# Mixture scores and values as fp32 products in quarters of the array, with exchanged halves and both tails together

## The chip, the cores and the metric

The kernel runs on one core of one Trainium2 chip. The metric is device time in microseconds: the median of three runs of the kernel before is 472.44 us (471.9 to 473.13). PE is TensorE, DVE is VectorE, ACT is ScalarE, POOL is GpSimd, and SP is the engine whose queue issues most of the loads and stores.

## The reference

Windowed attention (8 batches, 8 heads, 576 rows, head size 64), whose output is the input of a mixture of four causal attentions with gates:

```python
scores = scale * q @ k.T + slope[h] * -abs(i - j)      # attention: only 0 <= i - j < 128
x = softmax(scores) @ v                                # heads side by side: x is 576 x 512
logits = x @ w_gate                                    # the two largest of four get weights w
for e in range(4):                                     # mixture: experts of size 64
    q, k, v = x @ wq[e], x @ wk[e], x @ wv[e]
    a = softmax(causal(scale * q @ k.T))
    out += w[:, e] * (a @ v @ wo[e])                   # only where e is among the two
```

All inputs and outputs are fp32.

## The kernel before, in words

The 576 rows of a batch are four blocks of 128 and a tail of 64. Two heads, or two experts, make a pair, one in each half of the 128 partitions. Attention of a batch is four groups of two heads. Then the mixture of the batch runs: projections to Q and K (`qkproj`) and to V with the gates (`vproj`), scores of a pair (`moe_s`) and of its tail (`moe_s_tail`), norms and gate weights (`moe_norm`), transposes of the probabilities (`moe_t`), the product with V (`moe_pv`, `moe_pv_tail`), and the output product (`moe_wo`).

PE works with numbers in two ways. An fp32 product has two records in the trace for each instruction. An fp32r product is one record, and where its precision is not enough the kernel splits each factor into a high and a low part and adds three products (high by high, low by high, high by low): `WH`, `WL` for weights, `QH`, `QL`, `KH`, `KL` for Q and K, `AH`, `AL` for the result of `moe_pv`. The array is used whole (128*128), in two halves (64*128 by rows, 128*64 by columns) or in four quarters (64*64), and products on different parts of it run side by side. Quarters are used before in attention's scores and values; the mixture's scores are fp32r in row halves, the score tails fp32r on the whole array (through `QJ`, a block diagonal of two tails of Q), the mixture's values fp32 in column halves.

The helpers that choose an engine are `evac` (copy out of PSUM on ACT or DVE), `rnd` (rounding to fp32r on POOL or ACT), `ssub` (the low part, DVE or POOL) and `dve_sub` (the same out of PSUM, DVE only). All eight banks of PSUM are one pool (`ps`), SBUF tiles of one width another (`w5`: 1344 columns, `w4`: 1024, `w2`: 512); a tile takes the buffer that came free first in the final order.

The kernel first records all operations. `plan` then puts them in an order that is written out as a packed table (`ORDER`): it gives the place of every operation in one list, which of the alternative engines runs it, and where an idle product (`fill`) is put in on PE. `place` gives the buffers. Each engine runs its part of that list from first to last, and waits where a factor, a buffer or a bank is not ready. So every recorded operation has one line in the profile, L1189, and the clearing of the banks L1187.

At the start DVE clears part of each bank (192 columns of the upper 64 partitions), PE runs `fill` products into the banks (`warm`), and attention's scores of the first four groups begin as soon as their head data arrive; the four weight blocks (`wall`) are loaded behind the head data, rounded and split (`wprep`).

Of the kernel before, what the change touches and what calls it, by code (L numbers as in the profile page):

```python
# [20 lines left out]
DM = H * D  # L21
E = 4
# [8 lines left out]
BIG = 3.0e38  # L31
EPS = 1e-9
# [1244 lines left out]
```

## Time and profile before

| | |
|---|---|
| median of three runs | 472.44 us |
| the profiled execution's own time | 473.2 us |
| its span | 471.4 us |
| busy: PE, DVE, ACT, POOL | 462.7, 409.3, 370.5, 222.7 us |
| granted clock of PE, mean | 0.998 |

The span runs from the first to the last recorded work. A busy time is the union of the instructions of an engine; on PE they overlap, since a product's record runs from its first column to its last result, so a product's price is read from the distance of two starts and not from one record's length. An instruction's row gives what its engine waited for before it, in square brackets, where the wait was seen.

### The profile page before, as it was taken

The numbers are of one execution on the slowest core, as the hardware profiler recorded it, in microseconds if no ns is written. First come the engines' busy times: TensorE is split into PE (matmuls) and PEld (weight loads), VectorE is DVE, ScalarE is ACT, GpSimd is POOL, SyncE is SP. The second block draws the span as 40 slices with busy tenths as digits, with TensorE's granted clock in tenths as the row PEclk, the third lists the DMA queues.
The fourth block names the chain that finished last, engine by engine and source line by source line (L and its number), as shares of the span: only waits on it lengthen the run. The fifth ranks groups of instructions, "written<-read, shape, count | busy, mean of one in ns | idle before, by whom it ended". The sixth has DMA issues, their size and how long they took to land.

```text
span 471.4 us, 17542 instructions
## 1 busy us (share of the span) xinstructions
PE 462.7 (98%) x6380; PEld 403.8 (86%) x6380; DVE 409.3 (87%) x1894; ACT 370.5 (79%) x1409; POOL 222.7 (47%) x464
## 2 busy tenths in 40 slices
PE   7999999999999999999999999999999999999996
PEld 5788999897889789797898987898789897899775
DVE  6999999979998998879989798798999979966852
ACT  5968879989978688796989798897976959833952
POOL 4833968183916346261470907426263623561430
PEclk9999999999999999999999999999999999999999
DMA  7899410345320653150441281602731030300033
GB/s 202 266 221 246 112 52 1 77 103 141 108 80 0 139 142 117 29 140 1 115 129 37 80 189 39 180 2 61 205 121 38 3 86 2 120 1 1 3 113 112
DMA packets 29862, 44.99 MB, mean 95 GB/s; under 512 B 9424, under 2 KB 15824, under 8 KB 29776
## 3 DMA queue, kind: packets, MB, share of 16 engines
q1 hardware_dynamic: 29040, 43.42, 34.0%
q8 instruction: 50, 0.82, 0.8%
q10 hardware_dynamic: 736, 0.46, 0.4%
q14 instruction: 36, 0.29, 0.2%
HBM read 34.42 MB, written 9.44 MB: 93 GB/s over the span
## 4 chain that ended last, share of the span: by engine, by line
PE 84%; DMA 5%; SPq 3%; DVE 3%; ACT 2%; POOL 1%; issue 1%; DVEq 0%
PE ps L1189 84%; DMA w<-in_hd 4%; SPq L1189 3%; DVE w L1189 2%; ACT w L1189 2%; POOL w L1189 1%; DMA w<-in_wall 1%; DVE ps L1189 1%; DVE WL L1189 0%; DVE ALm L1189 0%; ACT AHm L1189 0%; DVE mr L1189 0%; DVE nm L1189 0%; POOL QJm L1189 0%; DVE ALTm L1189 0%
## 5 line engine op out<-in xcount | busy, mean ns | idle before, releaser
L1189 ACT COPY w<-ps 128x256 f32<-128x256 f32 (+2 forms) x232 | 92.4, 443 | 29.8 <-PE ps L1189 21.3
L1189 PE MATMUL ps<-wx,WH 128*128 128x288 f32 (+2 forms) x512 | 110.4, 300 | 0.0
L1189 ACT ACTIVATE w<-w,nm 128x128 f32<-128x128 f32 x252 | 98.9, 397 | 7.3 <-DVE nm L1189 5.8
L1189 POOL TENSOR_SCALAR w<-w,mr,w 128x256 f32<-128x256 f32 (+3 forms) x128 | 78.2, 622 | 43.2 <-DVE mr L1189 24.1
L1189 POOL TENSOR_SCALAR w<-w,r 128x128 f32<-128x128 f32 x177 | 64.6, 378 | 68.3 <-PE ps L1189 25.4
L1189 PEld LDWEIGHTS ps<-wx,WH 128*128 128x128 f32 x512 | 83.2, 190 | 1.5 <-issue 0.3
L1189 ACT ACTIVATE w<-w,mnm 128x512 f32<-128x512 f32 (+3 forms) x128 | 71.2, 558 | 10.0 <-DVE mnm L1189 9.4
L1189 DVE TENSOR_TENSOR w<-ps,tmt 128x768 f32<-128x768 f32 (+3 forms) x96 | 72.5, 770 | 3.3 <-PE ps L1189 2.2
L1189 DVE CUSTOM_DVE_ANT_0 w<-ps,tbt 128x128 f32<-128x128 f32 x288 | 71.7, 283 | 1.1
L1189 PE MATMUL ps<-wx,WL 128*128 128x288 f32 (+2 forms) x256 | 71.9, 298 | 0.0
L1189 PE MATMUL ps<-WH,wx 128*128 128x260 f32 x288 | 61.5, 285 | 0.0
L1189 PE MATMUL ps<-w 64*64 64x192 f32 (+3 forms) x1256 | 58.6, 304 | 2.3 <-DMA w<-in_hd 1.7
L1189 PE MATMUL ps<-idt,w 64*128 64x64 f32 (+1 forms) x1152 | 58.6, 230 | 1.0 <-POOL w L1189 0.9
L1189 PEld LDWEIGHTS ps<-idt,w 64*128 64x128 f32 (+1 forms) x1152 | 47.4, 139 | 11.0 <-issue 3.4
L1189 PE MATMUL ps<-w,vt 64*64 64x192 f32 (+3 forms) x1344 | 56.3, 283 | 0.0
L1189 PEld LDWEIGHTS ps<-w,vt 64*64 64x64 f32 (+1 forms) x1344 | 50.0, 133 | 5.7 <-DVE r L1189 0.6
L1189 DVE COPY_PREDICATED ps<-mkt,ps 128x128 f32<-128x128 int32 (+2 forms) x160 | 49.2, 329 | 5.4 <-PE ps L1189 5.0
L1189 PEld LDWEIGHTS ps<-w 64*64 64x64 f32 (+1 forms) x1256 | 44.0, 134 | 8.6 <-DMA w<-in_hd 2.7
L1189 DVE CUSTOM_DVE_ANT_0 w<-ps,mtt 128x256 f32<-128x256 f32 (+2 forms) x96 | 49.8, 551 | 0.8 <-PE ps L1189 0.4
L1189 PEld LDWEIGHTS ps<-WH,wx 128*128 128x128 f32 x288 | 48.0, 189 | 0.8 <-issue 0.3
L1189 ACT ACTIVATION_READ_ACCUMULATOR w<-w,nm 128x1 f32 x252 | 48.6, 193 | 0.0
L1189 PE MATMUL ps<-w,w 128*64 128x64 f32 (+4 forms) x576 | 48.0, 319 | 0.0
(111 smaller groups left out, 947.5 us busy)
## 6 DMA issues: line engine op xcount, KB each, us to landing
w<-in_hd SPq DMA_DIRECT2D x56, 288.0 KB, 4.6
vt<-in_vd SPq DMA_DIRECT2D x28, 320.0 KB, 3.7
out<-w SPq DMA_DIRECT2D x31, 256.0 KB, 2.5
w<-in_hd SPq DMA_DIRECT2D x14, 128.0 KB, 3.5
w<-in_hd SPq DMA_DIRECT2D x56, 32.0 KB, 3.7
w<-in_wall SPq DMA_DIRECT2D x4, 386.0 KB, 6.6
out<-w SPq DMA_DIRECT2D x8, 128.0 KB, 3.3
vt<-in_vd SPq DMA_DIRECT2D x4, 192.0 KB, 3.8
```

What stands on the lines that cost most here:

```text
L1189: getattr(getattr(tc.nc, e), m)(*a, **k)
```

## The change

Q and K of the mixture stay plain fp32 (`KK`), without high and low parts. Scores are single fp32 products in quarters: for block i, each half of 64 rows of Q runs only over the keys that it may see, so one half is 64 columns shorter than the other; in odd blocks the two halves are exchanged (`y ^ i & 1`), with a second mask table (`mts`) whose halves are exchanged too. The score tails of both pairs are one operation of each batch, fp32 in quarters. The transposes put the exchanged halves back (`spread`), the tails' transposes are five blocks in halves, and the gates' weights of odd blocks are computed with exchanged halves. `moe_pv` runs in quarters into two banks, whose sum is formed by a copy, an addition, a rounding and a subtraction; `moe_pv_tail` does so for both pairs at once. In attention's first half the first two blocks of a group run without wrapping (`first_blocks`). Pools change: `w5` has nine buffers for eight, `w4` six for four, `w2` five for six, `w1` goes. The weights are prepared in two parts each. The banks are cleared more widely, `ORDER` is another table (not shown), and the profile's lines become L1227 and L1224/L1225.

```diff
-    pp = big5 = _Slots(cp, 8, 2 * S + 3 * D, "w5")
+    pp = big5 = _Slots(cp, 9, 2 * S + 3 * D, "w5")
     tp = big10 = _Slots(cp, 3, 2 * (S + TAIL + S), "w10")
-    tw = _Slots(cp, 4, 2 * DM, "w4")
-    tr = _Slots(cp, 3, P, "w1")
-    big2 = _Slots(cp, 6, DM, "w2")
+    tw = _Slots(cp, 6, 2 * DM, "w4")
+    big2 = _Slots(cp, 5, DM, "w2")
...
+    mts = cp.tile([P, NQ * P], BF16, name="mts")
...
+    def first_blocks(g, ss, q, k, tb):
+        nm, sm, pt = state[g, 0]
+        for i in range(2):
+            n = P + P * i
+            for h in range(2):
+                d = slice(D * h, D * h + D)
+                for y in range(2):
+                    m = P * i + D * y
+                    nc.tensor.matmul(
+                        ss[h][D * y : D * y + D, P * i : P * i + n], q[h][d, m : m + D], k[d, :n], start=True, stop=True
+                    )
...
-    QJ = m1.tile([P, 2, 2, P], F32R, name="QJm")
     MPL = [m1.tile([P, (NQ + 1) * P], F32, name=f"MPL{k}") for k in range(2)]
-    QH, QL = (m1.tile([P, 2, S], F32R, name=f"{n}m") for n in ("QH", "QL"))
-    KK = m1.tile([P, 2, 2, S], F32R, name="KKm")
-    KH, KL = KK[:, 0], KK[:, 1]
+    KK = m1.tile([P, 2, 2, S], F32, name="KKm")
...
+    def terms(late):
+        return sorted(((c, j) for c in range(4) for j in range(3)), key=lambda z: late and z[1] == 2)
...
-        hi, lo = (QH, QL) if isq else (KH, KL)
-        act_copy(hi[:, pr, sl], o, n)
-        dve_sub(lo[:, pr, sl], o, hi[:, pr, sl].bitcast(F32), n)
-        if isq and half == 1:
-            for x, q in ((0, QH), (1, QL)):
-                for j in range(2):
-                    d = slice(D * j, D * j + D)
-                    pool_round(QJ[d, pr, x, d], q[d, pr, S - TAIL :].bitcast(F32))
+        evac(KK[:, 0 if isq else 1, pr, sl], o)
...
-        terms = ((QH, KH), (QL, KH), (QH, KL))
         o = 0
         jobs = []
         for i in blocks:
             n = P * (i + 1)
-            m = n if i else 2 * P
-            for x, (q, k) in enumerate(terms if i else terms[:2]):
-                for j in range(2):
-                    d = slice(D * j, D * j + D)
-                    k2 = k[d, pr, :n] if i else KK[d, :, pr, :P]
+            for j in range(2):
+                d = slice(D * j, D * j + D)
+                for y in range(2):
+                    m = P * i + D * (y ^ i & 1)
                     nc.tensor.matmul(
-                        ss[j][:, o : o + m], q[d, pr, P * i : P * (i + 1)], k2, start=(x == 0), stop=(x == (2 if i else 1))
+                        ss[j][D * y : D * y + D, o : o + m + D], KK[d, 0, pr, m : m + D], KK[d, 1, pr, : m + D], start=True, stop=True
                     )
-            if i == 0:
-                for j in range(2):
-                    nc.vector.tensor_tensor(st["pk", pr, j][:, :P], ss[j][:, :P], mtt[:, 512 - P : 512], add)
-                o += P
...
-                softmax_block(ss[j][:, o : o + n], pt, mtt[:, 512 - n : 512] if i else pt, nm[:, c : c + 1], n)
+                softmax_block(ss[j][:, o : o + n], pt, (mts if i % 2 else mtt)[:, 512 - n : 512], nm[:, c : c + 1], n)
...
-    def moe_s_tail(b, pr):
+    def moe_s_tail(b):
         st = m2s[b]
-        nm, sm = st[pr, "nm"], st[pr, "sm"]
-        pt = MPL[pr]
         ss = []
+        stats(b, 1)
         for half in range(2):
-            s = ps_s.tile([P, 512], F32, tag="s", name=f"msl{b}_{pr}_{half}")
-            ss.append(s)
+            ss.append([ps_s.tile([P, 512], F32, tag="s", name=f"msl{b}_{half}_{j}") for j in range(2)])
             sl = slice(HALF * half, HALF * (half + 1))
-            for k, (x, w) in enumerate(((0, KH), (1, KH), (0, KL))):
-                nc.tensor.matmul(s[:, :HALF], QJ[:, pr, x, :], w[:, pr, sl], start=(k == 0), stop=(k == 2))
...
+            for j in range(2):
+                d = slice(D * j, D * j + D)
+                for pr in range(2):
+                    nc.tensor.matmul(
+                        ss[half][j][D * pr : D * pr + D, :HALF], KK[d, 0, pr, NQ * P :], KK[d, 1, pr, sl], start=True, stop=True
+                    )
...
-    def moe_pv(b, pr, c):
+    def moe_pv(b, pr):
         st = m2s[b]
-        if c == 0:
-            st["acc"] = ps_a.tile([P, 512], F32, tag="m" if K["M"] else "a", name=f"ma{b}_{pr}", bufs=K["M"] or K["A"])
-        acc = st["acc"]
+        xa, ya = (ps_a.tile([P, 512], F32, tag="m", name=f"{n}{b}_{pr}") for n in ("ma", "mb"))
...
-        n = 512 - P * c
-        for j in range(2):
-            e = 2 * pr + j
-            nc.tensor.matmul(
-                acc[D * j : D * j + D, P * c :], V2[:, c, D * e : D * e + D], st["pt"][pr, j, c][:, :n],
-                start=(c == 0), stop=True, skip_group_check=True,
-            )
-        if c == NQ - 1:
-            act_copy(AH[:, pr, :512], acc, 512)
-            dve_sub(AL[:, pr, :512], acc, AH[:, pr, :512].bitcast(F32), 512)
-
-    def moe_pv_tail(b, pr):
+        for c in range(NQ):
+            for y, dst in enumerate((xa, ya)):
+                r, f = slice(D * y, D * y + D), D * y
+                for j in range(2):
+                    e = 2 * pr + j
+                    nc.tensor.matmul(
+                        dst[D * j : D * j + D, P * c + f :], V2[r, c, D * e : D * e + D], st["pt"][pr, j, c][r, f : 512 - P * c],
+                        start=(c == 0), stop=True, skip_group_check=True,
+                    )
+        tmp = big2.tile([P, DM], F32, tag="xs", name=f"ma{b}_{pr}t")
+        evac(tmp, xa)
+        nc.vector.tensor_tensor(tmp[:, D:], tmp[:, D:], ya[:, D:], add)
+        rnd(AH[:, pr, :512], tmp)
+        ssub(AL[:, pr, :512], tmp, AH[:, pr, :512].bitcast(F32))
+
+    def moe_pv_tail(b):
         st = m2s[b]
         pt = st["pt"]
         V2 = st["v2"]
-        acc = ps_t.tile([P, 512], F32, tag="t", name=f"mal{b}_{pr}")
+        ta, tb_ = (ps_t.tile([P, 512], F32, tag="t", name=f"mal{b}_{y}") for y in range(2))
         for c in range(NQ + 1):
-            for j in range(2):
-                e = 2 * pr + j
-                src = pt[pr, "tail", c][:, D * j : D * j + D]
-                nc.tensor.matmul(
-                    acc[D * j : D * j + D, :TAIL], V2[:, c, D * e : D * e + D], src,
-                    start=(c == 0), stop=(c == NQ),
-                )
+            for y, dst in enumerate((ta, tb_) if c < NQ else (ta,)):
+                r = slice(D * y, D * y + D)
+                for pr in range(2):
+                    for j in range(2):
+                        e = 2 * pr + j
+                        nc.tensor.matmul(
+                            dst[D * j : D * j + D, D * pr : D * pr + D], V2[r, c, D * e : D * e + D], pt[j, "tail", c][r, D * pr : D * pr + D],
+                            start=(c + pr == 0), stop=True, skip_group_check=True,
+                        )
         o = TAIL * (b % 2)
-        ht, lt = AHT[:, pr, o : o + TAIL], ALT[:, pr, o : o + TAIL]
-        act_copy(ht, acc[:, :TAIL], TAIL)
-        dve_sub(lt, acc[:, :TAIL], ht.bitcast(F32), TAIL)
+        ht, lt = AHT[:, :, o : o + TAIL], ALT[:, :, o : o + TAIL]
+        tt = p2.tile([P, P], F32, tag="xq2", name=f"xm{b}")
+        evac(tt, ta[:, :P])
+        nc.vector.tensor_tensor(tt, tt, tb_[:, :P], add)
+        v = tt.rearrange("p (a n) -> p a n", n=TAIL)
+        rnd(ht, v)
+        ssub(lt, v, ht.bitcast(F32))
...
             nc.sync.dma_start(mtt, mt)
+            for y in range(2):
+                nc.sync.dma_start(mts[D * y : D * y + D], mt[D - D * y : 2 * D - D * y, : NQ * P])
...
+            for f in (slice(0, 4 * P), slice(4 * P, NW)):
+                w, hi, lo = wst[c][:, f], WH[:, NP_ - 1 - c, f], WL[:, NP_ - 1 - c, f]
+                rnd(hi, w)
+                ssub(lo, w, hi.bitcast(F32))
+            return
...
-    fetch(0, 1, 0)
+    for g in range(4):
+        fetch(g, 1, 0)
     nc.scalar.dma_start(idt, ident)
-    nc.scalar.dma_start(tmt, tm)
-    nc.scalar.dma_start(mkt[:, P:], mk[:, P:])
...
     warm()
-    fetch(1, 1, 0)
     fetch_v(0, 0)
-    fetch(2, 2, 0)
     fetch_v(1, 0)
+    wload(0)
     fetch_v(2, 0)
-    wload(0)
     fetch_v(3, 0)
     for c in range(1, 4):
         wload(c)
+    nc.sync.dma_start(tmt, tm)
+    nc.sync.dma_start(mkt[:, P:], mk[:, P:])
...
+        moe_s_tail(b)
+        moe_norm(b, 0, 2)
+        moe_norm(b, 1, 2)
...
-        tc.nc.vector.memset(t[D:, : 3 * P].rearrange("p (a n) -> p a n", n=P)[:, :, :D], 0.0)
+        tc.nc.vector.memset(t[D:], 0.0)
+        tc.nc.vector.memset(t.rearrange("p (a n) -> p a n", n=4 * D)[:D, :, D : 2 * D], 0.0)
```

On SP, the order of loads at the start (`hd`: head data, `rd`: its query tails, `vd`: values, `mt`: mask table) begins before with

```order
L1189 DMA w_90<-in_hd 64x2x256 x4
L1189 DMA w_91<-in_hd 64x2x256 x4
L1189 DMA w_90<-in_hd 128x2x128
L1189 DMA w_90<-in_rd 128x2x320
L1189 DMA w_90<-in_hd 64x2x256 x2
```

and now with

```order
L1227 DMA mts<-in_mt 64x512 x2
L1227 DMA w_91<-in_hd 64x2x256 x4
L1227 DMA w_92<-in_hd 64x2x256 x4
L1227 DMA w_91<-in_rd 128x2x320
L1227 DMA w_91<-in_hd 64x2x256 x2
```

Two loads of the mask table stand ahead of all head data. The next rows of the same queue hold the four weight blocks (`in_wall`); before:

```order
L1189 DMA w_83<-in_wall 128x772
L1189 DMA vt_128<-in_vd 128x256
L1189 DMA vt_129<-in_vd 128x256
L1189 DMA w_86<-in_wall 128x772
L1189 DMA w_87<-in_wall 128x772
L1189 DMA vt_130<-in_vd 128x256
L1189 DMA vt_131<-in_vd 128x256
L1189 DMA w_88<-in_wall 128x772
```

and now:

```order
L1227 DMA vt_126<-in_vd 128x256
L1227 DMA vt_125<-in_vd 128x256
L1227 DMA w_83<-in_wall 128x772
L1227 DMA w_84<-in_wall 128x772
L1227 DMA mkt<-in_mk 128x64
L1227 DMA w_91<-in_hd 128x2x128
L1227 DMA vt_127<-in_vd 128x256
L1227 DMA vt_128<-in_vd 128x256
L1227 DMA w_85<-in_wall 128x772
L1227 DMA w_92<-in_rd 128x2x320
L1227 DMA w_92<-in_hd 128x2x128
L1227 DMA w_86<-in_wall 128x772
```

The fourth weight block was the 20th load of the queue and is the 25th.

On PE, a mixture pair's scores (blocks 3 and 2) in the middle of the program, with numbers of tiles and banks, before:

```order
L1189 MATMUL ps7_76<-KKm_125,QHm_123 128x512
L1189 MATMUL ps4_73<-KKm_125,QHm_123 128x512
L1189 MATMUL ps7_76<-KKm_125,QLm_124 128x512
L1189 MATMUL ps4_73<-KKm_125,QLm_124 128x512
L1189 MATMUL ps7_76<-KKm_125,QHm_123 128x512
L1189 MATMUL ps4_73<-KKm_125,QHm_123 128x512
L1189 MATMUL ps2_71<-KKm_125,QHm_123 128x384
L1189 MATMUL ps3_72<-KKm_125,QHm_123 128x384
L1189 MATMUL ps2_71<-KKm_125,QLm_124 128x384
L1189 MATMUL ps3_72<-KKm_125,QLm_124 128x384
L1189 MATMUL ps2_71<-KKm_125,QHm_123 128x384
L1189 MATMUL ps3_72<-KKm_125,QHm_123 128x384
```

and now, with the value product (`w41,w56`: probabilities and V) that stands behind it:

```order
L1227 MATMUL ps1_70<-KKm_122 64x512
L1227 MATMUL ps1_70<-KKm_122 64x448
L1227 MATMUL ps4_73<-KKm_122 64x512
L1227 MATMUL ps4_73<-KKm_122 64x448
L1227 MATMUL ps3_72<-KKm_122 64x320
L1227 MATMUL ps3_72<-KKm_122 64x384
L1227 MATMUL ps5_74<-KKm_122 64x320
L1227 MATMUL ps5_74<-KKm_122 64x384
L1227 MATMUL ps0_69<-w41_95,w56_88 64x512 x2
L1227 MATMUL ps7_76<-w41_95,w56_88 64x448 x2
L1227 MATMUL ps0_69<-w45_99,w56_88 64x384 x2
L1227 MATMUL ps7_76<-w45_99,w56_88 64x320 x2
```

Twelve products of 128 output rows became eight of 64, the longer half first in block 3 and second in block 2; the value product follows in the same tile size and takes two banks.

## Rows read from the trace of the kernel before

**Rows 1.** The page's first part: busy time, share of the span, instructions.

```profile
PE 462.7 (98%) x6380; PEld 403.8 (86%) x6380; DVE 409.3 (87%) x1894; ACT 370.5 (79%) x1409; POOL 222.7 (47%) x464
```

**Rows 2.** Busy time by stretch; columns: stretch, length, engines, clock, DMA share, GB/s.

```profile
0.00:25.00 25.00, 21.70 (x209) 17.23 (x209) 20.58 (x111) 17.40 (x71) 15.73 (x26) 1.00 0.84 236
...
100.00:200.00 100.00, 100.00 (x1503) 86.37 (x1504) 92.88 (x422) 81.73 (x305) 48.98 (x107) 1.00 0.35 92
200.00:300.00 100.00, 99.33 (x1406) 88.62 (x1399) 86.63 (x411) 85.69 (x331) 49.71 (x105) 1.00 0.36 95
300.00:400.00 100.00, 99.37 (x1405) 86.55 (x1405) 91.75 (x423) 81.26 (x315) 39.84 (x88) 1.00 0.26 74
```

**Rows 3.** The two holes: PE's timeline, then the chain (start, length, what).

```profile
284.45 0.60 PE L1189 MATMUL ps<-w 64*64 64x128 f32 x10 [0.67 <-DMA w<-in_hd]
...
335.05 4.65 DMA w<-in_hd
```

**Rows 4.** PE's timeline, quarters of attention; start, length, engine, operation, wait.

```profile
12.77 1.53 PE L1189 MATMUL ps<-w 64*64 64x192 f32 x32
14.23 0.87 PE L1189 MATMUL ps<-idt,w 128*128 128x128 f32 x5
```

**Rows 5.** PE's timeline, a pair's value product and what follows.

```profile
158.17 2.37 PE L1189 MATMUL ps<-w,w 128*64 128x512 f32 x16
160.47 0.33 PE L1189 MATMUL ps<-idt,w 128*128 128x128 f32 x1
...
160.91 0.29 PE L1189 MATMUL ps<-wx,WH 128*128 128x288 f32 x1
161.04 0.29 PE L1189 MATMUL ps<-KKm,QJm 128*128 128x288 f32 x1
```

**Rows 6.** PE's timeline, first score product of a pair and first work behind it.

```profile
217.83 0.50 PE L1189 MATMUL ps<-KKm,QHm 64*128 64x512 f32 x2
...
219.85 0.33 PE L1189 MATMUL ps<-idt,w 128*128 128x128 f32 x1
```

**Rows 7.** Groups by shape: busy us and mean ns, then idle before.

```profile
L1189 PEld LDWEIGHTS ps<-w 64*64 64x64 f32 x1248 | 42.8, 134 | 7.8 <-DMA w<-in_hd 2.7 <-issue 1.1 <-DVE G L1189 0.9
L1189 ACT COPY w<-ps 128x512 f32<-128x512 f32 x99 | 56.1, 590 | 16.2 <-PE ps L1189 15.4
L1189 POOL TENSOR_TENSOR wx<-w,wx 128x512 fp32r<-128x512 f32 x17 | 22.2, 1309 | 0.5
L1189 DVE TENSOR_TENSOR w<-w,ps 128x448 f32<-128x448 f32 x28 | 17.1, 612 | 1.2 <-ACT w L1189 0.6 <-PE ps L1189 0.2 <-issue 0.2
L1189 POOL TENSOR_SCALAR wx<-w 128x512 fp32r<-128x512 f32 x19 | 11.8, 624 | 27.5 <-DVE w L1189 23.1 <-ACT w L1189 3.7 <-DVE ps L1189 0.3
L1189 DVE TENSOR_TENSOR ALm<-ps,AHm 128x512 fp32r<-128x512 f32 x16 | 11.0, 686 | 1.1 <-ACT AHm L1189 0.8
L1189 DVE TENSOR_TENSOR wx<-w,wx 128x512 fp32r<-128x512 f32 x11 | 9.7, 877 | 1.2 <-ACT wx L1189 0.7 <-POOL wx L1189 0.4
L1189 ACT CAST AHm<-ps 128x512 fp32r<-128x512 f32 x14 | 8.1, 578 | 5.1 <-PE ps L1189 5.0
L1189 DVE MEMSET MPL<- 128x64 f32 x2 | 0.2, 112 | 0.0
```

**Rows 8.** The start, by engine: timelines of DVE, PE, SP and POOL.

```profile
0.85 1.67 DVE L1187 MEMSET ps<- 64x192 f32 x8 [0.85 <-PEq L1262]
...
1.30 3.57 PE L1189 MATMUL ps<-QJm 128*128 128x256 f32 x15 [1.30 <-DVE ps L1187]
4.81 3.69 PE L1189 MATMUL ps<-w 64*64 64x128 f32 x52
...
16.79 0.49 PE L1189 MATMUL ps<-wx,WH 128*128 128x256 f32 x2
...
0.73 5.97 SPq L1189 DMA_DIRECT2D w<-in_hd  x9
...
18.00 0.84 POOL L1189 TENSOR_SCALAR WH<-w 128x772 fp32r<-128x772 f32 x1 [0.65 <-DMA w<-in_wall]
```

More of the change, by code (lines that the diff above doesn't have):

```diff
@@ L31 @@
 BIG = 3.0e38
+NEG = -8.0e9
 EPS = 1e-9
@@ L312, in attn_moe_kernel @@
     prepped = {}
+    half = {}
     SM = [cp.tile([P, 9, 2], F32, name=f"sm{k}") for k in range(2)]
@@ L739, in qkproj, with stats @@
         o = acc[:, :n]
[L740 to L741 removed]
+        for k, (c, j) in enumerate(terms(b == 0 and half == 0)):
             xh, xl = xT[4 * b + c]
             cw = c if b else NP_ - 1 - c
[L744 to L757 removed]
+            lhs, rhs = ((WH, xh), (WH, xl), (WL, xh))[j]
+            nc.tensor.matmul(
+                o, lhs[:, cw, P * mtile : P * (mtile + 1)], rhs[:, n0:n1], start=(k == 0), stop=(k == 11)
+            )
+        sl = slice(n0, n1)
+        evac(KK[:, 0 if isq else 1, pr, sl], o)
+    def stats(b, pr):
+        st = m2s[b]
+        if (pr, "nm") not in st:
+            st[pr, "nm"] = m1.tile([P, 11], F32, tag=f"mnm{pr}", name=f"mnm{b}_{pr}")
+            st[pr, "sm"] = MSM[pr]
     def moe_s(b, pr, blocks):
@@ L761, in moe_s @@
         if blocks[0] == 0:
-            st[pr, "nm"] = m1.tile([P, 11], F32, tag=f"mnm{pr}", name=f"mnm{b}_{pr}")
-            st[pr, "sm"] = MSM[pr]
+            stats(b, pr)
             for j in range(2):
@@ new lines, in moe_s_tail @@
+            for j in range(2):
+                nm = st[j, "nm"]
+                bias = mtt[:, 0:HALF] if half == 0 else mtt[:, 512:]
+                init = BIG if half == 0 else nm[:, 9:10]
+                dst = nm[:, 9:10] if half == 0 else nm[:, 8:9]
+                softmax_block(ss[half][j][:, :HALF], MPL[j][:, sl], bias, dst, HALF, init=init)
+        for j in range(2):
+            nm, sm = st[j, "nm"], st[j, "sm"]
+            for half in range(2):
+                sl = slice(HALF * half, HALF * (half + 1))
+                exp_block(ss[half][j][:, :HALF], MPL[j][:, sl], nm[:, 8:9], sm[:, 16 + half : 17 + half], HALF)
+            st["p"][j, "tail"] = MPL[j]
@@ L836, in moe_t @@
         st = m2s[b]
-        parts = ([(0, 0), (1, 0)], [(0, 1), (0, 3), (1, 1), (1, 3)], [(0, 2), (1, 2)], [("tail", c) for c in range(NQ)])[u]
-        n = 8 if u < 2 else 4
-        pc = (tw if u < 2 else big2).tile([P, n * P], F32, tag="pt", name=f"mpt{b}_{pr}_{u}")
+        parts = ([(0, 0), (1, 0)], [(0, 3), (0, 1), (1, 1), (1, 3)], [(0, 2), (1, 2)], [("tail", c) for c in range(NQ + 1)])[u]
+        n = (8, 8, 4, 5)[u]
+        pc = (big2 if u == 2 else tw).tile([P, n * P], F32, tag="pt", name=f"mpt{b}_{pr}_{u}")
         blocks = []
@@ L943, in wload @@
             nc.sync.dma_start(mtt, mt)
+            for y in range(2):
+                nc.sync.dma_start(mts[D * y : D * y + D], mt[D - D * y : 2 * D - D * y, : NQ * P])
         wst[c] = w
@@ L1000, in f @@
             if tail:
-                moe_pv_tail(b, pr)
+                moe_pv_tail(b)
             else:
-                for c in range(NQ):
-                    moe_pv(b, pr, c)
+                moe_pv(b, pr)
             live[0] -= 0 if tail else 7
@@ L1127, in su @@
             else:
[L1128 removed]
+                u.append((0.1, early(lambda: first_norm(g))))
                 if g % 2:
```

328 lines of the change are left out of this document (162 added, 166 removed).

## The prediction

> **What bounds the kernel now.** I read the page's first part, then busy time in stretches, then TensorE's timeline. The first line says PE 98% busy, VectorE 87%, ScalarE 79%, GpSimd 47% [rows 1]. By stretches PE is busy 21.70 of the first 25 us, all of 100 to 200, 99.33 of 200 to 300 and 99.37 of 300 to 400, at a granted clock of 1.00 throughout, so at the upper of its two levels, 2.4 GHz [rows 2]. PE lists instructions as busy while they overlap, so 98% alone could hide gaps; but starts follow each other at the instructions' own rate, and outside the start only two holes show, of 0.67 and 0.63 us by the stretches, and both stand behind loads of head data [rows 2, 3]: the first is PE's wait at 284.45, the second is a load of 4.65 us on the chain of waits from 335.05. So the time is PE's work, plus what the first 25 us lose (3.30 us), plus 1.3 us of holes, plus what follows the last product. Shorter work on VectorE or ScalarE is worth nothing by itself.
>
> **Prices on PE.** Two rows give the fp32 price. The 32 records of 192 columns between 12.77 and 14.23 are 4 products for each quarter (two records each): 768 columns in 1.46 us [rows 4]. The 16 records of a value product between 158.17 and 160.47 run 512+384+256+128 = 1280 columns in each half: 2.30 us [rows 5]. The difference is 0.84 us for 512 columns, 1.64 ns a column, and leaves 0.20 us a stretch, which is what a change of tile size costs (going in and coming out). An fp32r step of 288 columns is 0.13 us (160.91 to 161.04) [rows 5]. One pair's fp32r scores, 11 steps, take 2.02 us from 217.83 to 219.85, so 1.82 without the change of size [rows 6].
>
> **The change, part by part (8 batches, 2 pairs each).**
> - Scores: each quarter now runs 512+320+256+64 or 448+384+192+128 = 1152 columns, 1.89 us against 1.82; 16 × 0.07 = +1.1.
> - The two quarters that write one bank differ by 64 columns in a block. If PE issues in order and every block ends with its longest, 128 columns a pair are lost, 0.21 us; if the shorter runs ahead, none. 0 to +3.4; I take +1.7, since the exchange makes the sums equal over two blocks but the queue need not reach that far.
> - Score tails: six steps for each pair were 2 × 6 × 0.13 = 1.56 us a batch; now 2 × 288 columns in four quarters, 0.94. 8 × -0.62 = -4.9.
> - Values: the busier row half still runs 1280 columns, and the tails ten times 64 for both pairs where each pair ran five: 0. The second bank only moves the sum of the halves to VectorE.
> - Attention's first half: 64 more columns a quarter in four groups, 4 × 64 × 1.64 ns = +0.4. The order of PE holds 32 more transposes of 64 columns and 8 fewer of 128, which I put at +0.2.
> - Tile sizes: scores, tails and values now stand side by side in one size; in the two orders of PE I count 153 changes of size before and 131 now. 22 × 0.20 = -4.4; some fall in the start, where PE waits anyway, so -4.0.
> Work on PE: +1.1 +1.7 -4.9 +0.4 +0.2 -4.0 = -5.5, with ends -7.2 and -3.8.
>
> **Other engines.** VectorE loses 64 subtractions of some 288 columns (each shorter than the 0.69 of a 512 wide one) and 32 additions of 128, and gets 16 additions of 448 at 0.61, 9.8 us, and part of 16 subtractions of 512; it becomes lighter by 20 to 30 us of 409. GpSimd gets up to 16 × (0.62 + 1.31) = 31 us on its 223, and ScalarE keeps its load within a few us [rows 1, 7]. All this lies beside PE and I cost it at nothing; the cover would be gone only where PE waits for one particular result (rival C).
>
> **The start.** It loses something at three places. (a) The clearing of banks: 8 × 192 columns were 1.67 us from 0.85. Now each bank clears 512 and 128. With 0.209 us at 192 and 0.112 at 64 a column costs 0.76 ns and an instruction 0.06, so 0.45 + 0.16 a bank, 4.9 us (bounds: 16 × 0.112 = 1.8 if the width costs little, 5.6 in proportion to 0.209), and each warm-up product waits for its own bank: the eighth starts at 5.8, it and the last six at 3.57/15 = 0.24 follow, and the first score comes near 7.4 instead of 4.81 [rows 7, 8]. (b) The load of the masks, twice, stands first on SP; nine issues took 5.97, so 0.66 each and 1.3 us for all loads behind. (c) The fourth weight block was SP's 20th load and is the 25th: 5 × 0.66 = 3.3 us later; GpSimd already waited 0.65 for such a block at 18.00 [rows 8]. Against this stands attention work of some 2 to 3 us that the new order puts ahead of the projections, which began at 16.79: it fills waits that the 3.30 us lost in the first 25 contain. Bounds: 0 (all the later arrivals are filled) to +4 (3.3 and some exponentials behind the first score). I take +2.0, the middle, for (c) alone is 3.3 and the filling is of its size.
>
> The holes of 1.3 us stay by my value; a ninth buffer for head data may remove them (rival E). The last chain, from the value product of the last tail to the output, has more steps now (below), but output products stand beside it: 0.
>
> **Sum.** -5.5 + 2.0 = -3.5 on the profiled execution, which took 473.2 us (span 471.4) and gives 469.7. It lay 0.8 us above the median of 472.44, so on that scale 468.9, rounded to 469.0.
>
> **Rivals.**
> B, the start eats it. The first score late by the full 2.6 us, the fourth weights by 3.3, and nothing to put between since ScalarE's exponentials of the first groups wait for those scores: +4 there, and PE work at its smaller end of -3.8: 472.6 on the median. For it: 21.70 of 25 us says PE already waits there. Against: wall waits are short (0.65), and order can be filled.
> C, slower: the results of value products become the wait. Before, a product left its bank by a copy of 0.58 and a subtraction of 0.69 and was ready, 1.27 us. Now it is a copy 0.59, an addition 0.61, a rounding 0.62 and a subtraction of 0.88 to 1.31: 2.7 to 3.1 [rows 7]. Two banks are held instead of one, and four for the score tails, of eight that transposes, scores and outputs share. If a third of those 1.4 to 1.8 us more shows at each of 16 value products and 8 tails, 24 × 0.5 = 12 us; at a tenth, 3.6. It decides from 0.15 us each (3.5/24). At 0.35 each, which I take for it: 472.4 - 3.5 + 8.4 = 477.3. For it: VectorE is at 93% in some stretches (92.88 of 100) [rows 2], so its queue is long. Against: it gets lighter, and output products stand between.
> The Trainium skill, "TensorEngine Tiling (Array Packing)", section PSUM Bottleneck, says the same in general: tiling speeds TensorE and not the copies out of PSUM, which may become the bound. No row of this kernel shows a product waiting for such a copy in the middle.
> D, the quarters don't run four at a time where two of them share rows, because the second one's weight load waits for the first one's product: a 64x64 load takes 0.134 us [rows 7], and a pair's scores have 16 products, 32 records, of which half would wait: 16 × 0.134 = 2.1 us a pair, 34 us in all, near 503. Against it: 32 such records fit into 1.46 us with their loads [rows 4]. Equal lengths there, unequal here, so 2 in 100 is left.
> The Trainium skill, "TensorE: Matmul & The Clock Gate", Part 3, states such a rule: a weight load overlaps a running product only when their row groups differ. Rows 4 speak against it here.
> E, more gain: the holes go (-1.3), the start costs nothing, and work is at -5.5: 473.2 - 0.8 - 6.8 = 465.6. For it: both holes are buffers that came free late.
>
> **Chances.** My forecast, 467 to 471, 0.46; E 0.13; B 0.20; C 0.19; D 0.02. Faster by over 0.3% (1.4 us, about what a measurement of this kernel can tell from no change) means below 471.0: the forecast's and E's parts, 0.59. Same, to 473.9: nearly all of B, and what C gives with less than 0.1 us each, 0.21. Slower: the rest of C and D, 0.20. The range of 8 in 10 is 464.5 to 475: E's end below, and above B with C from small prices on; C's own 477 and D lie outside.
>
> **What would show it.** In the new trace, one pair's scores in quarters should take 2.0 to 2.3 us with the change of size; above 2.4 the lengths cost more than I put. The score tails should take about 1.15 us a batch. The first score product should start between 7 and 8 us, and PE busy in the first 25 should be 20 to 22. From 100 to 400 PE should be without holes. I am wrong if holes with releaser VectorE or ScalarE of over 0.1 us stand behind value products (C), or if the start loses over 6 us (B).

## The result: 0.9% slower

The changed kernel took 476.56 us (median of 4 runs, 475.48 to 476.97) beside 472.17 for the kernel before in the same runs: ratio 1.0088 [1.0063, 1.0114]. Forecast were 469.0 and a gain; the range of 464.5 to 475 missed it. The profiled execution has a span of 474.5 us (before 471.4).

The first part of the page of the changed kernel, in the form of [rows 1]:

```profile
PE 464.2 (98%) x7106; PEld 403.7 (85%) x7106; DVE 394.2 (83%) x1843; ACT 364.0 (77%) x1380; POOL 240.7 (51%) x454
```

VectorE became lighter by 15 us (forecast 20 to 30), ScalarE by 6.5, GpSimd heavier by 18 (forecast up to 31). PE's busy time rose by 1.5 us where 5.5 less had been expected. The stretches of the changed kernel, columns as in [rows 2]:

```profile
0.00:25.00 25.00, 20.04 (x172) 14.10 (x173) 18.54 (x96) 14.06 (x54) 12.28 (x29) 1.00 0.83 237
100.00:200.00 100.00, 99.84 (x1639) 87.38 (x1641) 87.49 (x400) 82.38 (x314) 52.68 (x102) 1.00 0.34 93
200.00:300.00 100.00, 99.20 (x1558) 87.28 (x1550) 86.49 (x420) 82.51 (x318) 49.26 (x98) 1.00 0.34 89
300.00:400.00 100.00, 99.12 (x1678) 88.18 (x1671) 83.12 (x396) 78.14 (x298) 52.13 (x102) 1.00 0.26 73
```

PE lost 4.96 of the first 25 us (before 3.30), and 1.84 between 100 and 400 (before 1.30). By these rows the middle looks full, and that is the trap of this case: a PE instruction's end is modelled, and short waits vanish between overlapping records.

**The start.** VectorE's timeline of the changed kernel (start, length, what, idle time before), to be read beside [rows 8]:

```profile
0.92 0.48 DVE L1224 MEMSET ps<- 64x512 f32 x1 [0.92 <-PEq L1300]
1.50 0.17 DVE L1225 MEMSET ps<- 64x128 f32 x1
1.84 0.48 DVE L1224 MEMSET ps<- 64x512 f32 x1 [0.18 <-issue]
...
7.95 0.17 DVE L1225 MEMSET ps<- 64x128 f32 x1
```

and PE's:

```profile
2.64 0.58 PE L1227 MATMUL ps<-AHTm 128*128 128x256 f32 x1 [0.28 <-DVE ps L1225]
...
8.16 1.86 PE L1227 MATMUL ps<-AHTm 128*128 128x256 f32 x7 [0.34 <-DVE ps L1225]
9.96 0.71 PE L1227 MATMUL ps<-w 64*64 64x128 f32 x8
...
24.67 2.03 PE L1227 MATMUL ps<-wx,WH 128*128 128x256 f32 x13
```

A bank takes 0.92 us: 0.48 and 0.17 of clearing, the rest gaps. Every warm-up product waits for its bank, and the first score starts at 9.96 instead of 4.81. The first projection starts at 24.67 instead of 16.79, with attention work put ahead of it.

**The middle.** The waits before PE's weight loads, first of the kernel before, then of the changed one; columns: what waited, for whom, us in total, times, longest. These add up over waits that partly lie beside a running product, so only their shift is read.

```profile
PEld ps L1189 <- issue: 21.7, 94, 0.4
PEld ps L1189 <- POOL w L1189: 3.4, 11, 0.7
PEld ps L1189 <- DVE mnm L1189: 2.7, 10, 0.4
PEld ps L1189 <- DMA w<-in_hd: 2.7, 6, 0.8
PEld ps L1189 <- ACT w L1189: 2.4, 9, 0.4
PEld ps L1189 <- DVE w L1189: 1.8, 7, 0.6
```

```profile
PEld ps L1227 <- issue: 11.8, 54, 0.6
PEld ps L1227 <- DVE w L1227: 5.2, 15, 0.8
PEld ps L1227 <- ACT w L1227: 4.9, 18, 0.4
PEld ps L1227 <- DVE ps L1225: 4.4, 7, 0.6
PEld ps L1227 <- DVE mnm L1227: 3.0, 9, 0.7
...
PEld ps L1227 <- DVE ALm L1227: 0.5, 2, 0.4
```

The waits for head data are gone from the list, as rival E said. In their place stand results of VectorE and ScalarE (`w`: 1.8 + 2.4 before, 5.2 + 4.9 now) and the clearing (`ps L1225`). The low parts of the value results (`ALm`), the end of rival C's chain, are waited for only twice. Some of the waits point at banks: the loads for the scores read `KKm` alone, and still wait 1.6 us for ScalarE's copies into `w`, which empty banks. Before, no such wait was among the largest of this group:

```profile
L1189 PEld LDWEIGHTS ps<-KKm,QHm 64*128 64x128 f32 x224 | 21.2, 186 | 1.9 <-issue 0.7
```

```profile
L1227 PEld LDWEIGHTS ps<-KKm 64*64 64x64 f32 x640 | 28.7, 132 | 9.0 <-issue 1.6 <-ACT w L1227 1.6 <-DVE w L1227 0.8
```

### The profile page after: what moved, and what is told of

Read it like the earlier page. It is cut to its first block, busy times and chain, and to the rows that moved or that the text cites. A ratio compares the mean times of both kernels' runs of the same rounds, so it can differ in the third digit from the quotient of the medians.

```text
span 474.5 us, 18891 instructions
## 1 busy us (share of the span) xinstructions
PE 464.2 (98%) x7106; PEld 403.7 (85%) x7106; DVE 394.2 (83%) x1843; ACT 364.0 (77%) x1380; POOL 240.7 (51%) x454
## 4 chain that ended last, share of the span: by engine, by line
PE 84%; DVE 8%; issue 4%; POOL 3%; DMA 1%; ACT 0%; SPq 0%; POOLq 0%; DVEq 0%; ACTq 0%
PE ps L1227 84%; DVE w L1227 4%; POOL w L1227 2%; DVE ps L1227 1%; DVE ps L1224 1%; DMA out<-w 1%; DVE wx L1227 0%; DVE MPL L1227 0%; DVE r L1227 0%; DVE ps L1225 0%; DVE mr L1227 0%; POOL MPL L1227 0%; ACT wx L1227 0%; POOL AHm L1227 0%; DVE nm L1227 0%
## 5 line engine op out<-in xcount | busy, mean ns | idle before, releaser
L1227 ACT COPY w<-ps 128x512 f32<-128x512 f32 (+5 forms) x242 | 97.7, 450 | 36.7 <-PE ps L1227 28.2
L1227 POOL TENSOR_SCALAR w<-w,mr,w 128x512 f32<-128x512 f32 (+3 forms) x128 | 78.2, 621 | 62.6 <-DVE nm L1227 21.7
L1227 ACT ACTIVATE w<-w,nm 128x128 f32<-128x128 f32 x252 | 98.8, 396 | 9.9 <-DVE nm L1227 9.2
L1227 PE MATMUL ps<-wx,WH 128*128 128x288 f32 (+2 forms) x512 | 106.1, 301 | 0.2 <-DVE wx L1227 0.2
L1227 POOL TENSOR_SCALAR w<-w,r 128x128 f32<-128x128 f32 (+1 forms) x171 | 64.4, 388 | 66.6 <-DVE r L1227 30.7
L1227 PEld LDWEIGHTS ps<-wx,WH 128*128 128x128 f32 x512 | 81.4, 189 | 3.4 <-DVE wx L1227 0.5
L1227 ACT ACTIVATE w<-w,mnm 128x128 f32<-128x128 f32 (+3 forms) x128 | 71.0, 557 | 5.9 <-DVE mnm L1227 5.8
L1227 DVE TENSOR_TENSOR w<-ps,tmt 128x768 f32<-128x768 f32 (+2 forms) x92 | 68.9, 775 | 4.2 <-PE ps L1227 3.5
L1227 DVE CUSTOM_DVE_ANT_0 w<-ps,tbt 128x128 f32<-128x128 f32 x272 | 68.1, 283 | 0.8
L1227 PE MATMUL ps<-wx,WL 128*128 128x288 f32 (+2 forms) x256 | 67.4, 296 | 0.0
L1227 PE MATMUL ps<-w 64*64 64x192 f32 (+4 forms) x1256 | 63.6, 312 | 1.4 <-DVE nmA L1227 0.5
L1227 PE MATMUL ps<-w,vt 64*64 64x192 f32 (+5 forms) x1344 | 61.0, 283 | 0.1
L1227 PE MATMUL ps<-idt,w 64*128 64x64 f32 (+1 forms) x1160 | 59.1, 231 | 0.5 <-POOL w L1227 0.3
L1227 PEld LDWEIGHTS ps<-w,vt 64*64 64x64 f32 (+1 forms) x1344 | 52.3, 134 | 7.3 <-DVE w L1227 1.2
L1227 PE MATMUL ps<-WH,wx 128*128 128x260 f32 x288 | 58.1, 289 | 0.0
L1227 PEld LDWEIGHTS ps<-idt,w 64*128 64x128 f32 (+1 forms) x1160 | 48.2, 139 | 10.0 <-POOL w L1227 2.5
L1227 DVE COPY w<-ps 128x256 f32<-128x256 f32 (+5 forms) x104 | 44.9, 447 | 14.1 <-PE ps L1227 12.5
L1227 PEld LDWEIGHTS ps<-w 64*64 64x64 f32 (+1 forms) x1256 | 48.7, 137 | 8.4 <-DVE w L1227 1.4
L1227 PE MATMUL ps<-w,w 64*64 64x64 f32 (+7 forms) x1088 | 51.2, 308 | 0.5 <-issue 0.5
L1227 PE MATMUL ps<-KKm 64*64 64x288 f32 (+8 forms) x640 | 49.0, 412 | 0.0
L1227 DVE COPY_PREDICATED ps<-mkt,ps 128x256 f32<-128x256 int32 (+2 forms) x152 | 47.4, 332 | 1.9 <-PE ps L1227 1.4
L1227 ACT ACTIVATION_READ_ACCUMULATOR w<-w,nm 128x1 f32 x252 | 48.5, 192 | 0.0
```

What stands on the lines that cost most here:

```text
L1227: getattr(getattr(tc.nc, e), m)(*a, **k)
```

## Experiments

Two theories stood at first. S: the start costs it all. W: PE's own work did become shorter, but in the middle PE now waits for results of the other engines. A third, P, came up beside W: PE's own work is not shorter at all. All ratios are to the kernel before, run beside each experiment. The expectations have letters of their own: for the start, T is S (the clears make it late), L the loads, R waits in the middle that swallow the gain; for the middle, V is W with VectorE's queue as what is waited for, Q is W with the way of the value results; the S of e9 is the blocking of VectorE by GpSimd.

### The start

**e1: banks cleared by PE.** The memsets and the warm-up products are taken out; 16 products of a zeroed tile write the eight banks instead.

```diff
-    for t in ps_s.real:
-        tc.nc.vector.memset(t[D:], 0.0)
-        tc.nc.vector.memset(t.rearrange("p (a n) -> p a n", n=4 * D)[:D, :, D : 2 * D], 0.0)
+    seq_ = [x for x in seq_ if x is not nc.alt["fill"]]
...
+            for t in todo:
+                for f in range(0, 512, 256):
+                    tc.nc.tensor.matmul(t[:, f : f + 256], AHT[:, 0, :], ..., start=True, stop=True)
```

> The changed kernel, with the banks cleared by 16 products of zeros on TensorE instead of VectorE's 16 memsets and the 14 warm-up products. Theory T (the clearing makes the late start): VectorE spends 7.4 us on the clears before anything else and the first score starts at 9.96; here it starts near 5.5 to 6.5, and 3 to 4 us of the time go: 472.5 to 473.5. Rival L (the loads and the later weight blocks set the start): the first score is early, but the projections begin no more than 1 us sooner than 24.7, and the time stays within 1 us of 476.6. Rival R (waits in the middle swallow it): the start is better by 3 us and the end by less than 1.

**e2: the masks' loads (`mts`) behind those of `mtt` on SP**, and **e3: both edits.**

> The changed kernel, with the two loads of the second mask table moved on SP from the very front to behind the first mask table. Theory T: the first score waits for the clears, not for its data, so 476.6 stays within 0.5 us. Rival L: all loads come 1.2 us sooner and the time falls by 1.2 to 3 us.

> Both edits of the two runs before. Theory T: as the first alone, and up to 1 us better, since without the clears the data of the first scores is what is waited for: 471.5 to 473. Rival L: the sum of two effects, with most of it from the loads. What is then left over against a kernel with 4.4 us less work on TensorE (468) is the middle: 4 us.

**e4: the kernel before with nothing but the wide clears.**

> The kernel before, with only its clearing of the banks replaced by that of the change (64x512 and 64x128 for each bank). Theory T: the first score moves from 4.81 to about 9 and the time from 472.2 to 475 or 476. Rival L: the head start was not needed, the waits on loads and weights absorb it: below 473.2.

Measured: e1 472.30 us, 0.9996 [0.9982, 1.001]; e2 475.87, 1.0078 [1.0063, 1.0093]; e3 471.62, 0.9988 [0.9975, 1.0002]; e4 477.83, 1.012 [1.0101, 1.0138]. PE's start in e3:

```profile
1.10 3.78 PE L1235 MATMUL ps<-AHTm 128*128 128x256 f32 x16 [1.10 <-POOL AHTm L1231]
4.81 0.70 PE L1231 MATMUL ps<-w 64*64 64x128 f32 x8
```

and its stretches:

```profile
0.00:25.00 25.00, 23.02 (x231) 18.35 (x233) 18.14 (x100) 18.17 (x70) 17.18 (x36) 1.00 0.87 243
...
200.00:300.00 100.00, 98.93 (x1480) 87.02 (x1473) 85.29 (x403) 81.96 (x317) 54.18 (x105) 1.00 0.37 99
```

The first score is back at 4.81 and PE is busier in the first 25 us than before (23.02 against 21.70). The edit of the clears alone (e1) takes 0.9 points off the time, 4.3 us. So the clears are most of the start's loss; the masks' place is worth 0.1 points, 0.5 us, which the intervals do not tell from nothing. In e4 the clears alone cost 5.7 us, more than the 3 to 4 expected; there the granted clock fell too:

```profile
0.00:25.00 25.00, 18.58 (x162) 14.17 (x163) 17.97 (x103) 13.20 (x56) 10.71 (x23) 0.93 0.89 242
```

It is 1.00 in the changed kernel, with the same clears, so e4's price holds some clock as well and is an upper one. But S is not all: with the start mended the change gains 0.4 us (0.9988, not to be told from no change), not the 5.5 of the forecast's PE work.

### Is PE's own work shorter?

**e12 to e15: PE alone.** All of PE's instructions, in their order and with their shapes, on zeros; of the other engines only two-element copies are left, which keep the order in which banks are written and freed. e12 (of the kernel before) and e13 (of the changed one) have the banks cleared whole by VectorE and leave each copy on its own engine; e14 and e15 clear banks by 16 products, as e1, and share the copies evenly between VectorE and ScalarE. The warm-up products are left out in all four.

```diff
+        if e == "tensor":
+            getattr(tc.nc.tensor, m)(a[0], zeros(a[1]), zeros(a[2]), **k)
+        elif e in ("vector", "scalar"):
+            for x in a:
+                if isinstance(x, bass.AP) and x.tensor.name in banks:
+                    (copy of the first and last element of x)
```

> The kernel before with TensorE's products alone, in the same order, tiles and banks, on zeros (transposes with the identity); of VectorE's and ScalarE's instructions on PSUM only a copy of two elements a row is left, for the order of the banks, and no loads but the identity; the warm-up products are left out, and the outputs are zeros. By the price of its stretches without waits TensorE needs about 450 us, of which the start, the two holes behind loads and the rest of the waits (some 14 us) are absent.

> The same with the changed kernel's products. Theory W (TensorE's work fell as worked out from the rows, and the middle's loss is waiting): 4 to 6 us below the run before. Rival P (the quarters cost more on TensorE than worked out): within 1.5 us of it.

> TensorE alone with the products of the kernel before, as in the run on it above, but with 16 products of zeros at the start in place of VectorE's clears, and the small copies dealt out in turn to VectorE and ScalarE. With a start at 2.4 GHz some 462 to 466 us.

> The same with the changed kernel's products. Theory W (TensorE's work fell as worked out): 3.5 to 6 us below the run before. Rival P: within 1.5 us of it.

Measured: e12 473.01, far above the 450 expected, and e13 465.86, a pair that is not alike at its start (granted clock in the first 25 us 0.86 in e12, 1.00 in e13), so it settles nothing. e14 465.62, 0.9854 [0.9823, 0.9886], and e15 455.14, 0.9633 [0.9607, 0.9659], both at 1.00. The first lines of their pages:

```profile
PE 458.4 (99%) x6380; PEld 401.4 (87%) x6380; DVE 137.8 (30%) x844; ACT 138.0 (30%) x844; POOL 1.4 (0%) x5
```

```profile
PE 449.9 (99%) x7108; PEld 397.5 (88%) x7108; DVE 128.9 (28%) x788; ACT 129.0 (28%) x788; POOL 1.4 (0%) x5
```

and the waits for the small copies, of e14 and of e15:

```profile
PEld ps L1221 <- ACT w L1231: 7.2, 20, 1.5
PEld ps L1221 <- DVE w L1229: 4.5, 17, 0.4
```

```profile
PEld ps L1258 <- ACT w L1268: 4.2, 16, 0.7
PEld ps L1258 <- DVE w L1266: 3.5, 11, 0.8
```

PE's sequence became 10.5 us shorter, beyond W's 3.5 to 6; if all of the 4.0 us that these waits differ by is taken off, 6.5. The traces say that 10 is nearer: of every 20 products in turn I took the shorter of two times, in PE alone and in the whole kernel, so that a wait that only one of them has drops out; the sums are 453.4 us before and 443.3 now, 10.1 less. P falls: the forecast of -5.5 was too small. The pair also says what the full kernels lose against PE alone. PE's busy time is 462.7 against 458.4 before, 4.3 us of waits that the busy row counts as work, and 464.2 against 449.9 now, 14.3 us. To place them, I paired PE's products of a whole kernel and of PE alone in their order and read how much later the same product starts:

| us of PE alone | 20 | 100 | 160 | 220 | 280 | 340 | 440 | end of span |
|---|---|---|---|---|---|---|---|---|
| before, behind e14 | 0.9 | 1.3 | 1.7 | 2.2 | 1.7 | 3.4 | 4.4 | 7.6 |
| changed, behind e15 | 7.8 | 9.0 | 10.1 | 11.1 | 13.6 | 16.1 | 18.9 | 21.2 |
| e3, behind e15 | 2.7 | 4.7 | 5.8 | 7.1 | 9.2 | 11.3 | 13.7 | 15.9 |

The kernel before stays within some 2 us of PE's pace for 280 us. The changed one loses 8 us at the start and then falls back steadily, by 11 us to 440 where the kernel before loses 3.5; e3, with its start mended, does the same. So 7.5 us are lost in the middle, and W stands. Not all of it is seen as waits: between 25 and 440 us those that the list names before PE's loads (`issue` apart) rise by 4 us, from 14.7 before to 19.0 in e3.

### Who is waited for?

The longest waits of the middle stand at the turn to the fifth batch. PE's loads of the changed kernel:

```profile
289.87 0.20 PEld L1227 LDWEIGHTS ps<-w 64*64 64x64 f32 x4 [0.82 <-DVE w L1227]
290.60 0.36 PEld L1227 LDWEIGHTS ps<-w 64*64 64x64 f32 x10 [0.54 <-DVE mnm L1227]
```

VectorE ahead of them, then GpSimd at the same time:

```profile
286.46 0.45 DVE L1227 CUSTOM_DVE_ANT_0 MPL<-ps,mtt 128x288 f32<-128x288 f32 x1
...
286.95 1.23 DVE L1227 TENSOR_TENSOR w<-ex,ws 64x8 f32<-64x8 f32 x1
288.09 0.48 DVE L1227 COPY w<-ps 128x320 f32<-128x320 f32 x1
```

```profile
286.85 1.29 POOL L1227 TENSOR_TENSOR wx<-w,wx 128x512 fp32r<-128x512 f32 x1
```

VectorE has no pause here, and one tiny gate product of 64x8 takes 1.23 us where 13 of 16 such take about 0.17: it ends with GpSimd's subtraction, and the copies that PE needs queue behind it. All the following kernels are e3 with one more edit.

**e5: VectorE without the wraps**, 152 instructions in the trace (`copy_predicated`; the blocks concerned keep their unwrapped scores).

```diff
+    seq_ = [x for x in seq_ if x[1] != "copy_predicated"]
```

> The early-start version (clears by TensorE, masks late), with all 148 copies under a mask out of attention's scores left out: VectorE loses some 45 us, TensorE's work is the same; attention's scores of the wrapped blocks are not the reference's. The early-start version lies at 471.6, and its stretches of products after the first 25 us lose 4.5 us more than those of the kernel before. Theory V (these are waits for VectorE's queue): 3 us or more go, 468.5 or less. Rival P (quarters simply cost TensorE more than worked out): within 1 us of 471.6. Rival Q (the wait is the way of one value result through four steps, ScalarE and GpSimd included): within 1.5 us.

**e7: without the last step of the value results** (the low part `AL` is formed for batch 0 only).

```diff
+    al = [x for x in seq_ if x[1] == "tensor_tensor" and getattr(x[2][0], "tensor", None) is AA["AL"].tensor]
+    seq_ = [x for x in seq_ if not any(x is y for y in al[2:])]
```

> The early-start version, with the low part of the value results (the last of the four steps behind a value product) left out for all batches but the first, which leaves a stale low part in the output product. 14 subtractions of 0.75 to 1.29 us go, from VectorE 4 and from GpSimd 10. Theory Q (the longer way of a value result is what TensorE waits for): -2 us or more. Theory V: -0.5, by the 3 us that VectorE loses. Rival P: 0.

Measured: e5 470.25, 0.9966 [0.9951, 0.998]; e7 470.59, 0.9965 [0.9945, 0.9985]. VectorE's busy time fell from 389.2 in e3 to 356.4 in e5, for 1.4 us (e3's and e5's medians; their ratios differ by 0.2 points, 1.0 us). V had expected 3 us or more. Late waits stay where they were; e3 and then e5:

```profile
286.26 0.36 PEld L1231 LDWEIGHTS ps<-w 64*64 64x64 f32 x10 [0.55 <-DVE mnm L1231]
...
435.30 0.72 PEld L1231 LDWEIGHTS ps<-idt,w 64*128 64x128 f32 x16 [0.71 <-DVE mnm L1231]
```

```profile
285.56 0.36 PEld L1232 LDWEIGHTS ps<-w 64*64 64x64 f32 x10 [0.55 <-DVE mnm L1232]
...
434.64 0.72 PEld L1232 LDWEIGHTS ps<-idt,w 64*128 64x128 f32 x16 [0.71 <-DVE mnm L1232]
```

The same instructions wait for the same time with 33 us less on VectorE. So VectorE's load over the whole run does not set these waits. A queue just ahead of them is not excluded: no wrap stands there in e3 either, and VectorE works without a named wait in both kernels (in e5 from 283.05 to 286.37). That the result comes a fixed time after its product and PE has too little other work between fits, but is not shown. e7 takes rival C's own chain, the value results, one step shorter and gets about 1 us: as far as this step shows, that chain is a small part. C's banks (two held for one, four for the tails) no run varied, and the waits of the scores for ScalarE's copies point at them.

**Work moved between VectorE and GpSimd.** e6: the gates' small products on GpSimd; e8: e6 and all subtractions of the value results, their tails and `wx` on GpSimd. e9: only the first gate product of the fifth batch moved, behind two VectorE instructions. e10: e9 with the 11 low-part subtractions that GpSimd had on VectorE; e11: the 20 of `wx` as well.

```diff
-            nc.vector.tensor_tensor(wt[a, 1::2], ex[z, 1::2], ...)        # e6, e8
+            nc.gpsimd.tensor_tensor(wt[a, 1::2], ex[z, 1::2], ...)
...
+    i, j = (next(n for n, x in enumerate(seq_) if x is y) for y in gw[8:10])   # e9 to e11
+    seq_.insert(j - 1, seq_.pop(i))
```

> The early-start version, with the two small products of the gates' weights of each batch (64x2x4) on GpSimd instead of VectorE. One of the 16 took 1.23 us on VectorE instead of 0.17, from 286.95 to 288.18, while GpSimd ran a subtraction of 512 columns from 286.85 to 288.14. Theory V with that stall as a part: -1 us, 470.6. Rival: VectorE's queue is long for other reasons, less than 0.3 us; GpSimd's own place in its queue could delay the gates and cost up to 1.

> The early-start version with the gates' small products and all subtractions of 512 columns, of attention's result and of the value results, on GpSimd: VectorE loses 13 such and 16 small ones, some 12 us, GpSimd gains 19 on 242. Theory V: -1 to -2, since a lighter VectorE shortens its queue; if a result comes 0.5 us later each time and is waited for (theory Q), +1 to +3.

> The early-start version with one instruction moved: of the fifth batch's two small gate products on VectorE, the one that took 1.23 us instead of 0.17 beside GpSimd's subtraction goes two instructions down, next to the second one. Theory S (a product of two SBUF operands on VectorE waits until GpSimd's two-operand instruction has ended, and TensorE waits behind it at 285.5 and 286.3 for 0.84 and 0.55): the instruction takes 0.17 to 0.4 and the time falls by 0.7 to 1.1, to 470.7. Rival: the result there waits for something else that ends as late, within 0.3 us of 471.6.

> The run before with the last of the four steps behind the value products, 11 subtractions of 1.29 us on GpSimd, on VectorE at 0.75. Theory Q (TensorE waits for value results): -1 to -2 against it, since each comes 0.5 us earlier and GpSimd loses 14 us. Theory V (VectorE's queue is the wait): +0.5 to +2, for VectorE gains 8 us.

> The run before with also the 20 subtractions of 512 columns of attention's result on VectorE instead of GpSimd: GpSimd loses another 26 us, VectorE gains 16. The opposite step (all of them on GpSimd) cost 16 us. Theory Q, with GpSimd's queue as the slow part of the way: a further -1 to -3. Theory V: +2 to +6.

Measured: e6 473.64, 1.0051 [1.0032, 1.007]; e8 487.79, 1.0341 [1.0323, 1.0359]; e9 471.34, 0.9982 [0.9968, 0.9996]; e10 478.81, 1.0142 [1.0116, 1.0169]; e11 495.4, 1.0484 [1.0456, 1.0511]. What PE waits for in e8, then in e10:

```profile
PEld ps L1232 <- POOL w L1232: 10.5, 15, 2.6
...
PEld ps L1232 <- POOL wx L1232: 4.2, 3, 3.5
```

```profile
PEld ps L1240 <- DVE ALm L1240: 6.3, 5, 2.8
```

Both directions lose 2 to 24 us, far more than either theory expected (e6 -1 to +1, e8 -2 to +3, e10 -2 to +2, e11 -3 to +6 against e10): each move makes one in-order queue late for PE at a few places, by up to 3.5 us at once. In e8 and e11 the granted clock was 0.97 and 0.98 in two of the three stretches of 100 us between 100 and 400, so part of their loss is clock. e9 mends one stall; e3 and then e9:

```profile
285.52 0.20 PEld L1231 LDWEIGHTS ps<-w 64*64 64x64 f32 x4 [0.84 <-DVE w L1231]
```

```profile
285.49 0.20 PEld L1235 LDWEIGHTS ps<-w 64*64 64x64 f32 x4 [0.39 <-DVE w L1235]
```

The time falls by 0.3 us (medians), less than the 0.7 to 1.1 expected and not to be told from e3. It is the best version that leaves no work out, 0.2% under the kernel before, with an interval that just excludes no change. Which single chain would give back most of the middle's 7.5 us stays open: none that I shortened did, and neither the order of PE itself nor the number of banks held was varied.

## Why the prediction was wrong

The step that failed is "All this lies beside PE and I cost it at nothing". Lost there: e3, with the start mended, lags 11.0 us more at 440 than at 20, the kernel before 3.5 more; 7.5 us in place of 0. My reading is that the cover was PE's own work, and the change made that cover shorter while chains on the other engines stayed or grew; no run separates this from PE's new order or from the banks. The start, put at +2.0, is the second step. By the table the two spans differ by -10.5 of PE's work, +6.9 up to 20 us, +7.6 to 440 and -0.9 behind it: +3.1, as measured (474.5 against 471.4). Forecast were -5.5, +2.0, 0 and 0. That the miss is no larger is luck: PE's work fell by 5 us more than forecast and paid for part of the rest. Step by step:

- Work on PE, -5.5 with ends -7.2 and -3.8: measured -10.5 on PE alone, 10.1 by the shorter times. The sign holds, the size lies beyond the end of -7.2. By the distances of starts in e14 and e15 (copies' waits included), scores with tails take 46.0 us before and 40.9 now, 5.1 less where 2.1 were forecast; value products 46.7 and 44.1 (forecast 0), attention's products 99.2 and 96.7 (+0.4), transposes 52.3 and 51.7 (+0.2). The changes of size, put at -4.0, lie inside these and were not measured apart.
- The unequal lengths cost nearly nothing instead of +1.7. A pair's scores and value product took 219.40 to 223.65, 4.25 us. The busiest quarter has 1152 + 1280 = 2432 columns, 3.99 us at 1.64 ns, and a change of size is 0.20; that leaves 0.06, where a loss of 128 columns would add 0.21. The score tails came as put, 0.53 us for 288 columns a quarter, twice a batch:

```profile
219.40 1.74 PE L1227 MATMUL ps<-KKm 64*64 64x512 f32 x16
220.85 2.21 PE L1227 MATMUL ps<-w,w 64*64 64x512 f32 x30
...
223.65 0.53 PE L1227 MATMUL ps<-idt,MPL 64*128 64x64 f32 x10
...
287.59 0.72 PE L1227 MATMUL ps<-KKm 64*64 64x288 f32 x8
288.12 0.83 PE L1227 MATMUL ps<-w 64*64 64x128 f32 x22
```

- The start, +2.0 (0 to +4): +4.3 by e1, above its upper end. Step (a) put a bank at 0.61 us; it is 0.92, since I left out the gaps between the two clears and before the next bank. The last clear ends at 8.1 instead of 5.8, and the first score at 9.96 instead of 7.4 follows from that. Step (b), 1.3 us, is 0.5 by e2. Step (c) was not varied alone; with the clears gone the first 25 us are busier than before even with the masks in front (e1, 23.68 of 25).
- That "outside the start only two holes show" was read from busy rows. The list of waits of the kernel before, above, names more: `w`, `mnm` and others were waited for there too, and some of the 2.4 us behind `ACT w` are copies out of PSUM in the middle (at 216.01 a value product's load waits 0.28 us beside seven ScalarE copies `w<-ps`), so "No row of this kernel shows a product waiting for such a copy" was wrong.
- The holes of 1.3 us: rival E was right that they go, and wrong that this shortens the time, since PE then stands in other waits.
- The last chain, 0: the lag grows by 2.3 us from 440 to the end where it grew by 3.2 before, so nothing was lost there.
- Rivals: B had the place of one half (the start), at its +4. C's time (477.3) is the nearest, by luck in the number: its kind is right, waits for VectorE and ScalarE, but its main place is not, since a shorter way of the value results gave 1 us of 7.5; its banks stay open. D falls with the 4.25 us above, where waiting loads would have added 2.1.

On D, the Trainium skill, "TensorE: Matmul & The Clock Gate", Part 3, lets a weight load overlap a running product only when their row groups differ. In this trace quarters that share rows, with unequal lengths, ran within 0.06 us of the full overlap with one change of size, so the measurement decides against it here. The Trainium skill, "TensorEngine Tiling (Array Packing)", PSUM Bottleneck, warns that copies out of PSUM may become the bound when tiling speeds TensorE up. The trace agrees in direction: the waits for `w`, which such copies write among others, grew from 4.2 to 10.1 us.

## What to carry to other kernels

When an engine at 98% gets less work, its shorter work may also be less cover: price every result and every bank that it waits for again, by the distance in the order between producer and consumer, before the saving is booked. A busy row of overlapping records can hide 14 us of waits; a run of that engine alone, on zeros, shows them, and the lag behind it shows where. Preparation at the very start stands on the path even if it is a fill of a few hundred columns, so count the gaps between its instructions too.

## What the hardware showed that was not expected

- A VectorE product of 64x8 with both inputs in SBUF took 1.23 us instead of 0.17 while GpSimd ran a subtraction with two SBUF inputs, and ended 0.04 us behind it; in e9, moved by two places, it and the next one took 1.10 together, and the first again ended with that subtraction. The Trainium skill, "SBUF — State Buffer", Who interferes with whom, states it: two SBUF inputs on VectorE contend with a GpSimd instruction that reads SBUF, and the later one blocks for all of it. The trace agrees.
- Two clears of one bank on VectorE, 0.48 and 0.17 us long, come to 0.92 a bank. Sixteen products of zeros clear all eight banks in 3.78 us with no wait between.
- With the same wide clears the granted clock of the first 25 us was 1.00 in the changed kernel, the upper level of 2.4 GHz, and 0.93 in e4. In e4 it fell to 0.65 and 0.67 in the two stretches of 2.5 us from 15.0 to 20.0, behind one in which PE was busy for 1.11 of 2.5 us. In e12 it was 0.55, 0.50 (the lower level, 1.2 GHz) and 0.58 from 12.5 to 20.0, behind stretches with 1.03 of 2.5 us and, as it fell, 0.09. PE's busy time in the 25 us does not tell the runs apart: 18.58 in e4, and 18.08 in e13 at 1.00.
